# A larger head layout for transposes, a quotient of routing weights, and re-ordered first rounds and layer steps, in a kernel of attention followed by eight experts

## The chip, the cores and the metric

The kernel runs on one core of a Trainium2 chip. The metric is device microseconds (us) of one launch. A core has TensorE (PE in the profile: products, with weight loads on a row of their own, PEld), VectorE (DVE), ScalarE (ACT), GpSimd (POOL, which here mostly issues DMAs) and SyncE (SP, DMAs only). The engines run side by side, each through its own queue in order, and wait for each other by semaphores.

## The reference

Attention over 4 batches, 8 heads, 768 positions of width 64; heads 0, 2 and 6 see all earlier positions, the others only the first 4 and the last 64. The result, as 3,072 tokens of width 512, goes through a dense mixture of 8 experts (hidden width 1,024), weighted by a routing matrix P that is normalized by rows and columns eight times. Condensed:

```python
scores = scale * np.matmul(q, k.transpose(0, 1, 3, 2))
mask = np.where(retr[0, :, 0, 0, None, None], full_mask, stream_mask)
a = np.exp(np.where(mask, scores, -1e9) - max); a = a / a.sum(-1)
x = np.matmul(a, v).transpose(0, 2, 1, 3).reshape(B * S, H * D)
...
P = np.exp(x @ w_gate - max)
for _ in range(8):
    P /= P.sum(1, keepdims=True) + 1e-09
    P /= P.sum(0, keepdims=True) + 1e-09
    P *= N / E
for e in range(E):
    out += P[:, e:e + 1] * (np.maximum(x @ w1[e], 0.0) @ w2[e])
```

## The kernel before

Two stages follow each other, the first to about 177 us.

**Attention and expert 0.** A unit is a batch b, a third of its positions g (256 of them) and a half of the heads u (4 heads): 24 units. GpSimd loads k and q of (b, g) with a cast to 16 bits by `load_kq` (L90), as `[p, h, c, d]`: partition p holds positions 2p + c of each head h, so that a partition's run in memory is 2 x 64 numbers of one head. The first third of batch 0 comes by other queues in 32 bits and is rounded by ScalarE in `round_first` (L167). v of batch 0 comes in the same layout and is put in place by products and copies in `place_v` (L117); v of the other batches comes straight (`load_v_heads`, L133). `emit_prep` (L248) transposes k and q of a unit on TensorE: for each of k and q, pair of heads a and parity c, two products of 64 columns each, one for each head, into the two partition halves of a PSUM tile `tr`; VectorE copies that out as `kT`.

The work of a round is two tasks: scores (`emit_scores`, L427), exponent on ScalarE and mask on VectorE (the pair that `soften` runs), and a round later the sums over v (`gen_pv`, L281), normalized by VectorE into `xn`. `turn` (L312) transposes xn into xT with full products. As soon as xT has a third, expert 0's two layers for it are put in a list of fillers, which `fill` deals out among the rounds. Expert 0's output goes to `acc` unweighted, since P isn't known yet. The first six rounds (L527 to L582) are written out by hand, in the order in which PE, ScalarE and VectorE run them; `make_masks` (L231) builds the masks there, two VectorE operations for each pair of heads, and `warm` (L522) puts in products whose result isn't used. GpSimd's queue has its order by hand only at the start (L395 to L419); its later loads are placed by the planner as buffers come free.

Then P is normalized (L605 to L624), while fillers run.

**Experts 1 to 7.** 42 works (e, c), an expert and a chunk c of 512 tokens. The first work is plain (`layer1_plain`); in the other 41 `layer1` and `layer2` form a product of 2 x 2 blocks from seven block products (Strassen's scheme in Winograd's form): VectorE makes the sums of blocks (S1 and T2 of weights, T1 of xT, S2 of hT), TensorE the seven products, ScalarE copies a bank that is needed again to R (`copy`, L725; R1, R2 and R5, one buffer each), and VectorE adds and cuts at zero in `relu_sum`. A step (g, k) is product k for half g of the hidden width; the pairs at L761 set their order, a pair to a slot. In `layer2` the results times P of this expert go onto acc, by VectorE (L800) or by ScalarE and an adding DMA (L797, L805). `body` deals out slots: a pair of layer 1, a product of layer 2, and pieces of the other generators. `weight_first` (L638) is one of them: in expert 1 it multiplies acc by P of expert 0, four ScalarE operations of 128 x 512 for each chunk, before the first addition to that chunk. VectorE's order is by hand there; ScalarE's follows from the order of issue.

Of the kernel before, what the change touches and what calls it, by code (L numbers as in the profile page):

```python
# [10 lines left out]
F32 = mybir.dt.float32  # L11
# [25 lines left out]
def kernel(  # L37
# [49 lines left out]

    kq, vts = {}, {}

    def load_kq(b, g, h0=0, h1=H):  # L90
        if (b, g) not in kq:
            kq[b, g] = tuple(
                ap.tile([128, H, 2, D], F16, tag=n, bufs=3, name=f"{n}_{b}_{g}")
                for n in ("k16", "q16"))
        for src, dst in zip((k, q), kq[b, g]):
            nc.gpsimd.dma_start(
                out=dst[:, h0:h1].rearrange("p h c d -> p h (c d)"),
                in_=src[b, h0:h1, 256 * g:256 * g + 256, :].rearrange("h (p c) d -> p h (c d)", c=2),
            )

    def v_tile(b):
        if b not in vts:
# [14 lines left out]
    def place_v(g):  # L117

        for n in range(2):
            t = psA.tile([128, 512], F32, tag="mo", bufs=3, name=f"vp_{g}_{n}")  # L120
            rows = slice(64 * n, 64 * n + 64)
            for c in range(2):
                nc.tensor.matmul(
                    out=t[64 * c:64 * c + 64, :].rearrange("p (h d) -> p h d", h=H),
                    lhsT=ident16[rows, rows], rhs=vraw[g][rows, :, c, :], start=True, stop=True,
                )
            dst, src = v_tile(0)[:, :, 2 * g + n, 0:D], t.rearrange("p (h d) -> p h d", h=H)
            if g == 2:
                nc.vector.tensor_copy(out=dst, in_=src)
            else:  # L130
                nc.scalar.activation(out=dst, in_=src, func=AF.Copy, bias=0.0, scale=1.0)
# [34 lines left out]

    def round_first(h0):  # L167
        if (0, 0) not in kq:
            kq[0, 0] = tuple(ap.tile([128, H, 2, D], F16, tag=n, bufs=3, name=f"{n}_0_0")
                             for n in ("k16", "q16"))  # L170
        for i in range(2):
            nc.scalar.activation(out=kq[0, 0][i][:, h0:h0 + 4], in_=first32[:, i, h0:h0 + 4],
                                 func=AF.Copy, bias=0.0, scale=1.0)

    ret_u = constp.tile([128, 2 * H], U32, tag="ret_u")
# [55 lines left out]
    def make_masks(js):  # L231
        for h in [2 * j + hh for j in js for hh in range(2)]:
            nc.vector.tensor_scalar(
                out=masks[h // 2][:, h % 2, :], in0=keep, scalar1=over[:, h:h + 1],
                scalar2=None, op0=ALU.is_gt,
            )
# [11 lines left out]
    def emit_prep(b, g, u):  # L248

        tr = psA.tile([128, 512], F32, tag="mo", bufs=3, name=f"tr_{b}_{g}_{u}").bitcast(F16)  # L250
        for i, src in enumerate(kq[b, g]):
            for a in range(2):
                for c in range(2):
                    for hh in range(2):
                        nc.tensor.transpose(  # L255
                            out=tr[64 * hh:64 * hh + 64, ts(4 * i + 2 * a + c, 128)],
                            in_=src[:, 4 * u + 2 * a + hh, c, :], identity=ident16,
                        )
        t = ap.tile([128, 2, 2, 256], F16, tag=f"kT{u}{g}", bufs=1 + (g == 0),
                    name=f"kT_{b}_{g}_{u}")  # L260
        kTs[b, g, u], qTs[b, g, u] = t[:, 0], t[:, 1]
        nc.vector.tensor_copy(
            out=t.rearrange("r i a (n c p) -> r (i a) c n p", c=2, p=64),
            in_=tr.rearrange("r (i c n p) -> r i c n p", i=4, c=2, p=64),
        )
# [224 lines left out]
    def finish_sums(between=None):  # L490

        for i, ((gen, scale), key) in enumerate([(sums_of[key], key) for key in sums_of]):
            if i and between:
                between()
            while run(gen, 1):
                pass
            del sums_of[key]
            scale[0]()
# [15 lines left out]
    def scores(n):  # L514
        return [emit_scores(*t) for t in tasks[2 * n:2 * n + 2]]

    def soften(pairs, which=(0, 1)):
        for pair in pairs:
            for w in which:
                pair[w]()  # L520

    def warm(n):  # L522

        keep_warm(ident16, kTs[units[0]].rearrange("p a s -> p (a s)"), n)
# [3 lines left out]
    with tc.manual_schedule(engines=engines):  # L528
        keep_warm(blank[:, 0:128], blank, 9)
        make_keep()  # L530
        make_far()
        round_first(0)
        make_masks((0,))
        emit_prep(*units[0])
        make_masks((1,))
        round_first(4)
        r0 = scores(0)
        soften(r0, (0,))
        make_masks((2, 3))
        emit_prep(*preps.pop())  # L540
        warm(2)
        place_v(0)
        soften(r0, (1,))
        sum_later(0)
        r1 = scores(1)
        soften(r1, (0,))
        emit_prep(*preps.pop())
        finish_sums()
        r2 = scores(2)
        soften(r1, (1,))  # L550
        soften(r2, (0,))
        warm(2)
        turn()
        sum_later(1)
        r3 = scores(3)
        place_v(1)
        finish_sums(lambda: emit_prep(*preps.pop()))
        soften(r3, (0,))
        emit_vfar(0, 1)
        soften(r2, (1,))  # L560
        sum_later(2)
        turn()
        r4 = scores(4)
        finish_sums()
        soften(r3, (1,))
        soften(r4, (0,))
        fill(1)
        sum_later(3)
        finish_sums()
        soften(r4, (1,))  # L570
        fill(1)
        r5 = scores(5)
        turn()
        emit_prep(*preps.pop())
        soften(r5, (0,))
        spell_far(2, farx[:, :, 1])
        sum_later(4)
        finish_sums()
        fill(1)
        soften(r5, (1,))  # L580
        sum_later(5)
        fill(1)  # L582
# [15 lines left out]
    emit_logits(B - 1)  # L598
    late[0] = True

    rs = xp.tile([128, NB], F32, tag="rs")
    rr = xp.tile([128, NB], F32, tag="rr")
    bs = xp.tile([128, E], F32, tag="bs")
    rcs = xp.tile([128, E], F32, tag="rcs")
    for it in range(8):  # L605
# [12 lines left out]
        if it == 7:  # L618
# [16 lines left out]
    psB = ctx.enter_context(tc.tile_pool(name="psB", bufs=4, space=bass.MemoryType.PSUM,  # L635
                                         reuse_waits="tile"))

    def weight_first(c):  # L638

        for nb in range(4 * c, 4 * c + 4):  # L640
            nc.scalar.activation(out=acc_of(nb), in_=acc_of(nb), func=AF.Copy,  # L641
                                 bias=0.0, scale=Pne[:, nb, 0:1])
            yield

    works = [(e, c) for e in range(1, E) for c in range(NCH)]
    lefts1, rights1, lefts2, rights2, hTs = {}, {}, {}, {}, {}
# [60 lines left out]
    def layer1(e, c):  # L707
# [50 lines left out]
                                     bias=0.0, scale=1.0)  # L758


        for pair in (((0, 1), (0, 2)), ((0, 5), (0, 6)), ((0, 3), (1, 1)), ((0, 7), (1, 2)),  # L761
                     ((1, 5), (1, 6)), ((0, 4), (1, 7)), ((1, 3), (1, 4))):
            for g, k in pair:
                step(g, k)
            yield
# [8 lines left out]
    def layer2(e, c):  # L774
# [15 lines left out]
        def add(bank, i, n, by_dma):  # L790
            if by_dma:
                t = mp.tile([128, 2, 256], F32, tag="add", bufs=3, name="add")
            for q in range(2):
                dst = acc[c][:, i, n, q, :]
                w = Pne[:, 4 * c + 2 * q + i, e:e + 1]
                if by_dma:
                    nc.scalar.activation(out=t[:, q, :], in_=banks[bank][q], func=AF.Copy,  # L797
                                         bias=0.0, scale=w)
                else:
                    nc.vector.scalar_tensor_tensor(  # L800
                        out=dst, in0=banks[bank][q], scalar=w, in1=dst,
                        op0=ALU.mult, op1=ALU.add,
                    )
            if by_dma:
                nc.gpsimd.dma_start(out=acc[c][:, i, n, :, :], in_=t, accum_op=ALU.add)  # L805
# [51 lines left out]
    def body(n):  # L857
        e, c = works[n]
        if c == 0 and e + 1 < E:
            expw[e + 1] = load_expert(e + 1)  # L860
        if c == 2 and e + 1 < E:
            gens["w"] = combine_w(e + 1)
        if e == 1:
            gens["first"] = weight_first(c)
            gens["x"] = combine_x((c + 1) % NCH)
        for slot in range(7):
            go("l1", 2 if n == 0 and slot == 0 else 1)
            if slot in (1, 5):
                go("w")
                go("x", 2)  # L870
            go("l2")
            if slot in (2, 3, 5, 6):
                go("first")
            if slot in (2, 3):
                go("h")
            if n == 0 and slot == 0:
                run(combine_w(1), 9)
        if n + 1 == len(works):
            gens["l2"] = layer2_last(e, c)
            return  # L880
        gens["h"] = combine_h(e, c)
        go("h", 2)
        gens["l2"] = layer2(e, c)
        gens["l1"] = layer1(*works[n + 1])
# [40 lines left out]
```

The softmax here doesn't subtract the row's maximum and nothing guards it: scores larger than these inputs give would overflow.

## Time and profile before

| | us |
|---|---|
| median of 8 runs | 701.1 |
| lowest, highest | 700.51, 702.83 |
| the profiled execution, whole time | 700.68 |
| its span | 699.0 |

| group in the profile | what it is |
|---|---|
| L255 tr<-ident,k and tr<-ident,q | transposes of keys and queries, 192 products each, median 219 ns |
| L641 acc<-acc,Pne | acc times P of expert 0, ScalarE, 24 of them |
| L727 R<-l1y, R<-l1w | ScalarE's copies of a bank to R, about 600 ns |
| L718, L783 | products of layer 1 and layer 2 of experts 1 to 7 |
| L733 | VectorE's sum and cut at zero, about 685 ns |

Durations of products overlap, as they are pipelined; what a product takes of TensorE's time is read from one start to the next. The profile's clock row shows TensorE's full clock granted all through.

### The profile page before, as it was taken

The page shows a single profiled execution, that of the slowest core. Times are in us where ns is not written, and L with a number is a line of the kernel's source. Part 1 is how long each engine was busy: PE and PEld are TensorE (multiplying, and loading weights), DVE is VectorE, ACT ScalarE, POOL GpSimd, SP SyncE. Part 2 cuts the span into 40 slices and gives each one's busy share as a digit, 9 for nine tenths or more (in the row PEclk, how much of TensorE's full clock was granted, in tenths as well). Part 3 has the DMA queues.
Part 4 walks back from the last instruction along what each step waited for, and adds up shares of the span by engine and source line. Part 5 has one row for each costly group of instructions (what it writes and reads, how often), then busy time and mean ns, then how long its engine had stood idle before and what let it go on. Part 6 is the DMA issues. An engine that isn't in the chain of part 4 may idle for free.

```text
span 699.0 us, 17004 instructions
## 1 busy us (share of the span) xinstructions
PE 684.3 (98%) x6913; PEld 568.6 (81%) x6913; DVE 570.1 (82%) x1149; ACT 419.9 (60%) x775; POOL 151.2 (22%) x183
## 2 busy tenths in 40 slices
PE   7999999999999999999999999999999999999997
PEld 3666666666588888888888888888888888888885
DVE  7785665757889988888888878988898788888785
ACT  6777677774896555655555565555556555555651
POOL 7432220000012131212212121122212212121210
PEclk9999999999999999999999999999999999999999
DMA  9999691000734287346924594349433964245785
GB/s 179 183 192 130 50 76 14 3 1 2 120 61 76 48 129 128 63 76 111 147 47 76 93 151 77 61 68 163 88 62 61 144 114 77 46 76 108 144 163 148
DMA packets 84256, 65.62 MB, mean 94 GB/s; under 512 B 48336, under 2 KB 64720, under 8 KB 84176
## 3 DMA queue, kind: packets, MB, share of 16 engines
q0 software_dynamic: 74976, 57.17, 58.7%
q1 hardware_dynamic: 7552, 6.30, 3.7%
q10 hardware_dynamic: 1648, 1.05, 0.6%
q8 instruction: 54, 0.88, 0.5%
q14 instruction: 26, 0.21, 0.1%
HBM read 52.45 MB, written 6.29 MB: 84 GB/s over the span
## 4 chain that ended last, share of the span: by engine, by line
PE 92%; ACT 4%; DVE 2%; issue 1%; DMA 1%; ACTq 0%
PE l1y L718 20%; PE l2y L783 20%; PE l1w L718 10%; PE l2w L783 10%; PE l L375 6%; PE l1z L718 5%; PE l2z L783 5%; PE l L361 5%; PE sc L454 3%; PE pv L291 3%; ACT PT L463 2%; PE tr L255 2%; PE last L835 1%; PE l1b L698 1%; PE xt L320 1%; ACT acc L641 1%
## 5 line engine op out<-in xcount | busy, mean ns | idle before, releaser
L805 POOL DMA_DIRECT2D acc<-add x120 | 101.4, 845 | 381.0 <-DVE hT L733 182.8
L718 PEld LDWEIGHTS <-S 128*128 128x128 f16 x1312 | 128.3, 98 | 17.2 <-issue 2.1
L783 PEld LDWEIGHTS <-S 128*128 128x128 f16 x1312 | 128.3, 98 | 14.9
L727 ACT ACTIVATE R<-l1y 128x512 f32<-128x512 f32 x164 | 98.5, 601 | 40.5 <-PE l1y L718 40.5
L800 DVE SCALAR_TENSOR_TENSOR acc<-l2y,Pne,acc 128x256 f32<-128x256 f32 x248 | 108.1, 477 | 18.0 <-PE l2y L783 17.9
L718 PEld LDWEIGHTS <-w 128*128 128x128 f16 x984 | 96.3, 98 | 11.4
L783 PEld LDWEIGHTS <-hT 128*128 128x128 f16 x984 | 96.3, 98 | 11.1
L718 PE MATMUL l1y<-T,S 128*128 128x256 f16 x656 | 98.4, 273 | 0.5 <-ACT R L727 0.5
L463 ACT ACTIVATE PT<-sc 128x1024 f16<-128x1024 f32 (+1 forms) x96 | 82.9, 922 | 12.9 <-PE sc L454 12.3
L783 PE MATMUL l2y<-T,S 128*128 128x256 f16 x656 | 85.0, 273 | 0.0
L797 ACT ACTIVATE add<-l2z,Pne 128x256 f32<-128x256 f32 x80 | 33.6, 472 | 77.2 <-PE l2z L783 77.2
L727 ACT ACTIVATE R<-l1w 128x512 f32<-128x512 f32 x82 | 49.2, 599 | 37.6 <-PE l1w L718 37.6
L655 DVE TENSOR_TENSOR S<-hT 128x1024 f16<-128x1024 f16 x82 | 56.2, 686 | 16.4 <-ACT hT L757 14.0
L733 DVE CUSTOM_DVE_ANT_0 hT<-l1w,R 128x512 f16<-128x512 f32 x82 | 56.1, 684 | 7.8 <-PE l1w L718 7.8
L733 DVE CUSTOM_DVE_ANT_0 hT<-l1z,R 128x512 f16<-128x512 f32 x82 | 56.1, 685 | 7.5 <-ACT R L727 7.4
L733 DVE CUSTOM_DVE_ANT_0 hT<-l1y,R 128x512 f16<-128x512 f32 x82 | 56.3, 687 | 4.3 <-PE l1y L718 0.8
L757 ACT ACTIVATE hT<-l1y 128x512 f16<-128x512 f32 x82 | 49.1, 599 | 17.2 <-PE l1y L718 16.0
L797 ACT ACTIVATE add<-l2w,Pne 128x256 f32<-128x256 f32 x80 | 33.6, 472 | 28.1 <-PE l2w L783 27.2
L718 PE MATMUL l1w<-xT,S 128*128 128x256 f16 x328 | 49.2, 273 | 1.1 <-ACT R L727 1.1
L718 PE MATMUL l1y<-xT,w 128*128 128x256 f16 x328 | 49.2, 273 | 0.0
L718 PE MATMUL l1z<-xT,w 128*128 128x256 f16 x328 | 49.2, 273 | 0.0
L718 PE MATMUL l1w<-T,S 128*128 128x256 f16 x328 | 49.2, 273 | 0.0
(106 smaller groups left out, 1043.7 us busy)
## 6 DMA issues: line engine op xcount, KB each, us to landing
acc<-add POOLq DMA_DIRECT2D x120, 256.0 KB, 3.4
w<-in_moe_w_dram POOLq DMA_DIRECT2D x16, 1024.0 KB, 10.4
out_dram<-acc SPq DMA_DIRECT2D x43, 128.0 KB, 2.8
k<-in_k_dram POOLq DMA_DIRECT2D x11, 256.0 KB, 10.7
q<-in_q_dram POOLq DMA_DIRECT2D x11, 256.0 KB, 11.5
v<-in_v_dram POOLq DMA_DIRECT2D x12, 192.0 KB, 11.5
acc<-in_v_dram POOLq DMA_DIRECT2D x3, 256.0 KB, 7.6
acc<-in_q_dram ACTq DMA_DIRECT2D x2, 256.0 KB, 5.4
```

What stands on the lines that cost most here:

```text
L361: nc.tensor.matmul(out=l1[:, ts(fb % 2, 256)], lhsT=w1[:, dc, ts(fb, 128)], rhs=xT[dc // 2][:, dc % 2, c0:c0 + 256], start=(dc == 0), stop ...
L375: nc.tensor.matmul(out=l2, lhsT=hT[fc // 2][:, o:o + 128], rhs=w2[:, fc, :], start=(fc == 0), stop=(fc == 7),)
L463: nc.scalar.activation(out=PT[:, :, c0:c0 + width], in_=sc[:, :, 0:width], func=AF.Exp, bias=0.0, scale=SCALE,)
L655: nc.vector.tensor_tensor(out=out_, in0=a_, in1=b_, op=op)
L718: nc.tensor.matmul(out=banks[g, bank][:, f, :], lhsT=lefts1[e][k - 1][:, dc, ts(2 * g + f, 128)], rhs=rights1[c][k - 1][:, dc, :], start=( ...
L727: nc.scalar.activation(out=R[name], in_=banks[g, bank], func=AF.Copy, bias=0.0, scale=1.0)
L733: nc.vector._custom_dve(TENSOR_ADD_SAT, out=block(g, i, n), in0=banks[g, bank], in1=R[name], s0=65504.0, s1=0.0)
L757: nc.scalar.activation(out=block(g, 1, 0), in_=banks[g, "y"], func=AF.Relu, bias=0.0, scale=1.0)
L783: nc.tensor.matmul(out=banks[bank][q], lhsT=lefts2[e, c][k - 1][:, q, f, :], rhs=rights2[e][k - 1][:, f, :], start=(first and q == 0 and f ...
L797: nc.scalar.activation(out=t[:, q, :], in_=banks[bank][q], func=AF.Copy, bias=0.0, scale=w)
L800: nc.vector.scalar_tensor_tensor(out=dst, in0=banks[bank][q], scalar=w, in1=dst, op0=ALU.mult, op1=ALU.add,)
L805: nc.gpsimd.dma_start(out=acc[c][:, i, n, :, :], in_=t, accum_op=ALU.add)
```

## The change

There are four parts.

1. k and q of all thirds but the second and third of batch 0 are laid out as `[p, c, h, d]`, two heads side by side for each parity. `emit_prep` then transposes two heads by one product of 128 columns. A partition's run in memory becomes 64 numbers. The two thirds left out (`long_runs`) keep layout and products.
2. The first rounds by hand are re-ordered: masks of the last pair later, `place_v(0)` after the scores of round 1, `place_v(1)` before `turn`, the exponents of round 1 apart, one `warm` product in place of four. Of `place_v`'s copies the second (n = 1) goes to VectorE for all thirds.
3. With expert 1, acc isn't multiplied by P of expert 0. Instead expert 1's results are weighted with P1/P0 (`over0`), and acc is multiplied by P0 when expert 2 comes to the chunk. VectorE copies the weights for that to a small tile `wt`, and ScalarE's four operations stand in slots 1 and 2 of expert 2's chunks, one and three.
4. In `layer1` the third and fourth pairs of steps are (1,1), (1,2) and (0,7), (0,3) in place of (0,3), (1,1) and (0,7), (1,2).

```diff
+    def long_runs(b, g):
+        return b == 0 and g in (1, 2)
+
+    def kq_tiles(b, g):
+        shape = [128, H, 2, D] if long_runs(b, g) else [128, 2, H, D]
...
+            if long_runs(b, g):
+                nc.gpsimd.dma_start(out=dst.rearrange("p h c d -> p h (c d)"),
+                                    in_=s.rearrange("h (p c) d -> p h (c d)", c=2))
+            else:
+                nc.gpsimd.dma_start(out=dst, in_=s.rearrange("h (p c) d -> p c h d", c=2))
...
-            if g == 2:
+            if g == 2 or n:
                 nc.vector.tensor_copy(out=dst, in_=src)
...
+                    h, n = 4 * u + 2 * a, 4 * i + 2 * a + c
+                    if not long_runs(b, g):
+                        nc.tensor.transpose(
+                            out=tr[:, ts(n, 128)], identity=ident16,
+                            in_=src[:, c, h:h + 2, :].rearrange("p h d -> p (h d)"),
+                        )
+                        continue
...
         round_first(4)
         r0 = scores(0)
         soften(r0, (0,))
-        make_masks((2, 3))
+        make_masks((2,))
         emit_prep(*preps.pop())
-        warm(2)
+        warm(1)
+        soften(r0, (1,))
+        r1 = scores(1)
+        r1[0][0]()
         place_v(0)
-        soften(r0, (1,))
+        r1[1][0]()
         sum_later(0)
-        r1 = scores(1)
-        soften(r1, (0,))
         emit_prep(*preps.pop())
         finish_sums()
+        make_masks((3,))
         r2 = scores(2)
         soften(r1, (1,))
         soften(r2, (0,))
-        warm(2)
+        place_v(1)
         turn()
         sum_later(1)
         r3 = scores(3)
-        place_v(1)
         finish_sums(lambda: emit_prep(*preps.pop()))
...
+    def weigh_over():
+        nc.vector.reciprocal(out=over0[:, :, 0], in_=Pne[:, :, 0])
+        nc.vector.tensor_tensor(
+            out=over0[:, :, 1:], in0=Pne[:, :, 1:LATE],
+            in1=over0[:, :, 0:1].broadcast_to([128, NB, LATE - 1]), op=ALU.mult)
+
+    def weight_of(e, nb):
+        return (over0 if e < LATE else Pne)[:, nb, e:e + 1]
...
-        for nb in range(4 * c, 4 * c + 4):
-            nc.scalar.activation(out=acc_of(nb), in_=acc_of(nb), func=AF.Copy,
-                                 bias=0.0, scale=Pne[:, nb, 0:1])
-            yield
+        wt = mp.tile([128, 4], F32, tag="wt", name=f"wt_{c}")
+
+        def hold(i0, i1):
+            nc.vector.tensor_copy(out=wt[:, i0:i1], in_=Pne[:, 4 * c + i0:4 * c + i1, 0])
+
+        def weigh(i0, i1):
+            for i in range(i0, i1):
+                x = acc_of(4 * c + i)
+                nc.scalar.activation(out=x, in_=x, func=AF.Copy, bias=0.0, scale=wt[:, i:i + 1])
+
+        hold(0, 1)
+        yield
+        weigh(0, 1)
+        yield
+        hold(1, 4)
+        yield
+        weigh(1, 4)
+        yield
...
-        for pair in (((0, 1), (0, 2)), ((0, 5), (0, 6)), ((0, 3), (1, 1)), ((0, 7), (1, 2)),
+        for pair in (((0, 1), (0, 2)), ((0, 5), (0, 6)), ((1, 1), (1, 2)), ((0, 7), (0, 3)),
...
-                w = Pne[:, 4 * c + 2 * q + i, e:e + 1]
+                w = weight_of(e, 4 * c + 2 * q + i)
...
+        if e == LATE:
+            gens["first"] = weight_first(c)
         if e == 1:
-            gens["first"] = weight_first(c)
             gens["x"] = combine_x((c + 1) % NCH)
         for slot in range(7):
+            if slot in (1, 2):
+                go("first")
             go("l1", 2 if n == 0 and slot == 0 else 1)
+            if slot in (1, 2):
+                go("first")
...
-            if slot in (2, 3, 5, 6):
-                go("first")
...
             if n == 0 and slot == 0:
                 run(combine_w(1), 9)
+                weigh_over()
```

More of the change, by code (lines that the diff above doesn't have):

```diff
@@ L88, with load_kq @@
     kq, vts = {}, {}
[L90 to L94, printed above, removed]
-        for src, dst in zip((k, q), kq[b, g]):
[L96 to L99, printed above, removed]
+    def long_runs(b, g):
+        return b == 0 and g in (1, 2)
+    def kq_tiles(b, g):
+        shape = [128, H, 2, D] if long_runs(b, g) else [128, 2, H, D]
+        kq[b, g] = tuple(ap.tile(shape, F16, tag=n, bufs=3, name=f"{n}_{b}_{g}")
+                         for n in ("k16", "q16"))
+    def load_kq(b, g):
+        kq_tiles(b, g)
+        for src, dst in zip((k, q), kq[b, g]):
+            s = src[b, :, 256 * g:256 * g + 256, :]
+            if long_runs(b, g):
[3 more added lines that the diff above has]
+                nc.gpsimd.dma_start(out=dst, in_=s.rearrange("h (p c) d -> p c h d", c=2))
     def v_tile(b):
@@ L168, in round_first @@
         if (0, 0) not in kq:
-            kq[0, 0] = tuple(ap.tile([128, H, 2, D], F16, tag=n, bufs=3, name=f"{n}_0_0")
-                             for n in ("k16", "q16"))
+            kq_tiles(0, 0)
         for i in range(2):
-            nc.scalar.activation(out=kq[0, 0][i][:, h0:h0 + 4], in_=first32[:, i, h0:h0 + 4],
+            nc.scalar.activation(out=kq[0, 0][i][:, :, h0:h0 + 4].rearrange("p c h d -> p h c d"),
+                                 in_=first32[:, i, h0:h0 + 4],
                                  func=AF.Copy, bias=0.0, scale=1.0)
@@ L253, in emit_prep @@
                 for c in range(2):
+                    h, n = 4 * u + 2 * a, 4 * i + 2 * a + c
[5 more added lines that the diff above has]
+                        continue
                     for hh in range(2):
                         nc.tensor.transpose(
-                            out=tr[64 * hh:64 * hh + 64, ts(4 * i + 2 * a + c, 128)],
-                            in_=src[:, 4 * u + 2 * a + hh, c, :], identity=ident16,
+                            out=tr[64 * hh:64 * hh + 64, ts(n, 128)],
+                            in_=src[:, h + hh, c, :], identity=ident16,
                         )
@@ L599 @@
     late[0] = True
+    LATE = 2
+    over0 = xp.tile([128, NB, LATE], F32, tag="over0")
     rs = xp.tile([128, NB], F32, tag="rs")
```

## The prediction

> **What bounds the kernel now.** I read the page first, then a table by stage, then the chain of waits and the timelines where a stage leaves TensorE idle.
>
> The page (busy time by engine, the slices, the chain that ended last):
> ```profile
> PE 684.3 (98%) x6913; PEld 568.6 (81%) x6913; DVE 570.1 (82%) x1149; ACT 419.9 (60%) x775; POOL 151.2 (22%) x183
> ...
> PE   7999999999999999999999999999999999999997
> ...
> DMA  9999691000734287346924594349433964245785
> ...
> PE 92%; ACT 4%; DVE 2%; issue 1%; DMA 1%; ACTq 0%
> ```
> TensorE is the bound: 684.3 of 699.0 us. There are two ways to gain: fewer or shorter products, or some of the 14.7 us in which it idles. The DMA row is full only for the first 70 us or so.
>
> The table of stages (columns: stretch, length, busy time and instructions of PE, PE's weight loads, VectorE, ScalarE, GpSimd; clock; DMA share; GB/s):
> ```profile
> 0.00:30.00 30.00, 24.13 (x300) 14.52 (x301) 23.31 (x64) 20.02 (x29) 17.26 (x27) 1.00 1.34 183
> 30.00:60.00 30.00, 29.13 (x456) 19.77 (x455) 22.74 (x58) 23.36 (x33) 11.61 (x13) 1.00 1.94 179
> 60.00:90.00 30.00, 29.31 (x429) 20.09 (x426) 19.26 (x48) 21.10 (x31) 9.07 (x10) 1.00 1.17 76
> 90.00:150.00 60.00, 59.43 (x843) 40.15 (x844) 38.55 (x97) 44.94 (x62) 1.77 (x3) 1.00 0.24 22
> ...
> 189.00:201.00 12.00, 11.50 (x105) 10.02 (x104) 9.83 (x20) 12.00 (x25) 2.60 (x3) 1.00 0.26 45
> 201.00:213.00 12.00, 11.76 (x108) 10.31 (x106) 11.82 (x25) 9.77 (x19) 2.42 (x4) 1.00 0.35 62
> 213.00:225.00 12.00, 12.00 (x112) 10.77 (x110) 11.81 (x25) 6.97 (x14) 2.30 (x4) 1.00 0.37 63
> ...
> 300.00:690.00 390.00, 390.00 (x3565) 348.55 (x3564) 334.61 (x614) 215.48 (x440) 85.34 (x101) 1.00 0.57 98
> ```
> Idle time lies in the first 30 us (5.87) and round the start of expert 1. There ScalarE has not a moment free (12.00 of 12), while from 201 VectorE is at 98%. From 300 on PE has no gap at all.
>
> The chain of waits from 186 to 196 (start, us, what):
> ```profile
> 186.35 1.61 ACT acc L641 x3
> ...
> 189.15 1.22 ACT acc L641 x2
> ...
> 190.86 2.06 ACT acc L641 x4
> ```
> and PE's timeline at the stalls there, and at the largest one that the change touches in the start:
> ```profile
> 188.72 0.60 PE L718 MATMUL l1w<-xT,S 128*128 128x256 f16 x4 [0.84 <-ACT R L727]
> 195.05 0.60 PE L718 MATMUL l1y<-T,S 128*128 128x256 f16 x4 [0.50 <-ACT R L727]
> 202.12 0.60 PE L718 MATMUL l1w<-xT,S 128*128 128x256 f16 x4 [0.24 <-ACT R L727]
> ...
> 20.09 0.28 PE L320 MATMUL xt<-ident,xn 128*128 128x128 f16 x2 [0.75 <-DVE xn L305]
> ```
> In all three stalls a product waits for ScalarE to copy a bank (R), and ahead of that copy stand the scalings of acc at L641.
>
> The key and query transposes and, for the full size, those of xn (x8 and x4 are products in the line):
> ```profile
> 130.15 0.41 PE L255 MATMUL tr<-ident,k 128*64 128x128 f16 x8
> 130.39 0.39 PE L255 MATMUL tr<-ident,q 128*64 128x128 f16 x8
> 130.72 0.30 PE L291 MATMUL pv<-vf,PT 128*128 128x65 f16 x4
> ...
> 133.48 0.40 PE L320 MATMUL xt<-ident,xn 128*128 128x128 f16 x4
> 133.72 0.28 PE L291 MATMUL pv<-vf,PT 128*128 128x65 f16 x4
> ```
> From start to start, 16 half-size ones take 130.72 - 130.15 = 0.57 us (36 ns each), 4 full-size ones 0.24 us (60 ns each).
>
> **What the Trainium skill says.** "TensorE: Matmul & The Clock Gate", Part 3: Packing small matmuls, lets small products in different parts of the array run side by side. The trace agrees: a 128-column product of half width advances by 36 ns, a full one by 60. So the 16 halves are not worth 16 full ones, and halving the count doesn't halve the time. The same page, Part 1: The HAM clock gate, has the clock at half until a window of some 3.4 us was busy; here the first transposes last 316 ns and later ones 219. "DMA: Bandwidth & Descriptors", Specifications, asks for at least 512 B per transfer for line rate. The trace agrees in direction: a 256 B packet of k takes 41 ns, a 128 B packet of v 32, so bytes cost more in small packets. "Perfetto Trace Analysis", DVE / Act Engine Instruction, shows a wait queue ahead of the execution FIFO, so a waiting instruction holds what follows; the copies of R behind L641 are that case.
>
> **The change part by part.**
>
> *Full-size transposes.* 20 of 24 units lose 16 half products for 8 full ones: 160 products fewer. 8 x 60 ns = 0.48 against 0.57 us: 0.09 us a unit. Two units lie in the start, which other waits set; 18 follow where PE is 97 to 99% busy, so 18 x 0.09 = 1.6 us. Unknown: xn's products may not have k's pace. Bounds 0.04 and 0.12 a unit (0.7 to 2.2 us); it is nothing if a full one costs what a pair costs, 71 ns. VectorE's copy of tr is unchanged.
>
> Price: each changed k or q DMA goes from 1,024 packets of 256 B to 2,048 of 128 B. v's 1,536 such packets land about 1.55 us apart when the engines are full, k's 1,024 about 1.43; so 2,048 take about 2.07, +0.65 us a DMA. On POOL's queue the order is the old one but for v's second load of batch 1, now behind k and q of the next third, and w2 of expert 1, behind the k and q after that (5 us of transfer out of their way). Landing and first use before: first k, q of batch 1 at 30.5 and 31.9 against 36.1; v by 40.8 against VectorE's 45.4; the third k, q 51.7 and 53.2 against 56.0; everything later over 10 us early. With +0.65 each the tightest land near 33.2, 43.4 and 52.0: cost 0. Issuing one takes GpSimd 0.88 us (k) or 0.96 (v); by that slope 2,048 take some 1.05, with GpSimd 22% busy. If a DMA takes over 0.9 more, the third pair is late, by up to 1 us.
>
> *First rounds.* The last mask pair goes 0.7 us of VectorE later, behind two copies of keys; two v copies move from ScalarE (0.59) to VectorE (0.69); three warm products go; place_v(0) goes behind the scores of round 1, place_v(1) ahead of turn. The wait at 20.09 is set by VectorE's queue (keys' copy, masks, v copy, reciprocal, xn). Into it come one 0.69 copy and out of it go two masks; ScalarE is relieved of 0.6 in front of the exponents. I take 0.1 us gained, bounds -0.4 (gain 0.4) and +1.5: with the warm products gone, a gap of some 0.3 us near 11.5 can make the clock rise one window later. w2 of expert 0, which lands at 28.7 and is used at 29.5, caps a gain at 0.8.
>
> *Expert 1 over expert 0's weight.* 24 scalings at L641 of 0.7 to 0.8 us leave the six chunks of expert 1 for those of expert 2; 12 short VectorE copies (two per chunk) and two operations for the quotient are added. Start to start the three stalls are: 188.72, where the eight products begun at 186.84 end their pace (0.87) at 187.71, so 1.0; 195.05 against 193.95 + 0.44, 0.66; 202.12 against 200.85 + 0.87, 0.40. Sum 2.1. With two or three scalings of 0.6 (start to start) out from ahead of each R copy, these are covered. What is late next is VectorE, which has gaps of 2.0 at 183.9 and of 0.8, 0.8, 0.4 at 195 to 200 to catch up in. I take 2.0 gained, bounds 0.5 and 2.1. In expert 2 ScalarE has a gap of 2.02 us per chunk (at 301.7) and needs 3 x 0.6 there: nothing. The fourth, in front of R1 of the second half, puts that some 0.4 us back, and what waits is a VectorE sum with slack.
>
> *Order of layer 1's steps, 41 chunks.* Product 3 of the first half moves 2.2 us later. Its sum must read R2 before ScalarE writes R2 again, now one slot on: by the steady chunk it ends near 304.6 and the copy starts at 304.91, slack 0.28; in the full chunks of expert 1 it is 0.03. PE has no idle time there to win: gain 0, cost 0 while VectorE stays in time; I put 0.1 in for expert 1.
>
> Sum on the profiled execution's 700.68 us (699.0 span, 1.7 round it): -1.6 - 0.1 - 2.0 + 0.1 = -3.6, so 697.1. That execution lies 0.4 under the median of 701.1, so for the median 697.5.
>
> **Rivals.** 0.2% (1.4 us) is about what a measurement can tell from no change.
> - A. Full-size transposes cost what pairs do, because the strip of two heads is read at a longer stride or its weight load (106 ns on its own engine) shows. For: 60 ns is four products' pace only. Against: weight loads have room there (40.15 of 60). 701.1 - 2.0 = 699.1.
> - B. VectorE takes over between 185 and 250: it is at 11.8 of 12 from 201, so PE catches up into it and gives back 1.9 of the 2.0. Against: its own gaps before 201. 701.1 - 1.7 = 699.4.
> - C (slower). The single R2 buffer: VectorE's sum of product 3 is later than ScalarE's copy wants, and R2's copy, its bank and the next product wait. It repeats in all 41 chunks, where PE has no slack: 0.15 us each is 6.2, so 701.1 - 3.6 + 6.2 = 703.7. It decides from 0.12 us a chunk. For: the slack is 0.28 and VectorE 86% busy there. Against: VectorE waits for PE 0.2 to 0.4 us several times a chunk, so it recovers.
> - D. The start loses: half clock one window longer, or packets dearer than 0.9 us a DMA. 1.5 to 3.5 lost of the 3.6: 699 to 701.
> That the change does not do what it says I rule out by the instructions: the 160 transposes are gone and the scalings stand in expert 2.
>
> **How the numbers follow.** The likeliest case (gains of 2.5 to 4.6, 696.5 to 698.6) 0.58, A 0.10, B 0.11, C 0.11, D 0.10. Range 696.0 to 700.4: down to all gains at their upper bound, up through A, B and half of D; C and the rest stay out. Faster by over 0.2% (under 699.7): 0.58 + 0.08 + 0.07 + 0.05 = 0.78. Within: 0.02 + 0.04 + 0.05 + 0.01 = 0.12. Slower: C, 0.10.
>
> **What would show it.** Transposes: eight products from the first of tr to the next pv in about 0.48 us; in 60 to 150 us the same work ends some 1.5 us sooner. Expert 1: no idle of PE over 0.3 us from 188 to 203, and ScalarE under 11 of 12 there. Layer 1: PE still without a gap from 300 on, a chunk still every 12.2 us; a wait of an R2 copy or of l1w there would be C. Start: xn's second half at or before 20.1. Wrong would be: a transposing product above 70 ns, an engine other than PE at 100% from 189 to 225, or a wait of PE for k, q or kT between 30 and 60.

## The result, and the profile after

The changed kernel takes 696.73 us (median of 10 runs, 696.53 at the lowest) against 701.12 before (28 runs): a ratio of 0.9938, 95% interval 0.9929 to 0.9946, so 4.3 us faster (3.8 to 5.0). Two later sets of five runs gave 697.88 and 697.08. The forecast was 697.5. One of the ten, the one that was profiled, took 1,005 us with TensorE's clock at 0.658 of full speed, so the lines below are from a later execution of the same kernel (697.0 us, span 695.1).

The page of the changed kernel:

```profile
PE 681.2 (98%) x6750; PEld 568.5 (82%) x6750; DVE 575.8 (83%) x1165; ACT 421.4 (61%) x773; POOL 157.9 (23%) x183
...
PE   6999999999999999999999999999999999999997
...
PEclk7999999999999999999999999999999999999999
DMA  9999791000633396437834593349433954245685
...
PE 93%; ACT 3%; DVE 2%; DMA 1%; issue 1%; SPq 0%; DVEq 0%; ACTq 0%
```

163 products are gone, and TensorE is still the bound. Its first slice went from 7 to 6, and its clock row now opens with a 7: in this execution the clock stood at half until 18.0 us. The table of stages of the changed kernel, with columns as before:

```profile
0.00:30.00 30.00, 23.55 (x279) 14.73 (x280) 23.77 (x66) 18.96 (x27) 18.08 (x26) 0.83 1.39 181
30.00:60.00 30.00, 29.10 (x420) 19.99 (x419) 23.11 (x60) 23.96 (x34) 14.50 (x14) 1.00 2.31 170
...
90.00:150.00 60.00, 59.30 (x792) 40.42 (x792) 39.48 (x98) 46.48 (x63) 2.50 (x2) 1.00 0.30 21
...
189.00:201.00 12.00, 12.00 (x112) 10.75 (x111) 11.33 (x23) 6.96 (x14) 2.61 (x3) 1.00 0.37 67
201.00:213.00 12.00, 12.00 (x112) 10.75 (x111) 11.73 (x25) 6.97 (x14) 2.51 (x3) 1.00 0.37 67
213.00:225.00 12.00, 12.00 (x111) 10.65 (x110) 11.71 (x25) 7.08 (x14) 2.53 (x3) 1.00 0.36 66
...
300.00:690.00 390.00, 390.00 (x3551) 347.22 (x3550) 335.98 (x611) 217.28 (x442) 85.35 (x101) 1.00 0.57 100
```

Round the start of expert 1 ScalarE fell from 12.00 to 6.96 of 12 us, and the table shows no idle time of TensorE from 189 on. (Busy times of pipelined products overlap, so pauses of about 0.1 us don't show in it; they are read below from one start to the next.) VectorE went up there from 9.83 to 11.33 and still keeps pace.

To see where the time went, the same events are compared in the traces (us against the kernel before; minus is earlier). Each column is one execution. The 3rd to the 6th copy of kT belong to the two thirds that keep the old layout; l2z is a bank of layer 2's products, so its 17th product lies in expert 1 and its 65th in expert 2:

| event | time before | layout alone | rounds alone | weights alone | step order alone | changed, 1st | changed, 2nd |
|---|---|---|---|---|---|---|---|
| 3rd copy of kT | 14.26 | -0.52 | -0.70 | +0.08 | +0.46 | -0.37 | +0.34 |
| 7th copy of kT | 36.87 | -0.52 | -0.09 | +0.08 | +0.46 | -0.49 | +0.31 |
| start of expert 1 (first hT<-l1b) | 178.40 | -2.78 | -0.08 | +0.10 | +0.46 | -2.74 | -1.93 |
| 17th product of l2z | 217.04 | -2.77 | -0.08 | -2.18 | +0.57 | -5.02 | -4.22 |
| 65th product of l2z | 290.40 | -2.77 | +0.01 | -2.09 | +0.88 | -4.60 | -3.81 |
| first product of the last layer | 687.78 | -2.76 | +0.02 | -2.08 | +0.89 | -4.59 | -3.80 |
| end of the span | 698.97 | -2.77 | -0.10 | -2.08 | +0.87 | -3.01 | -3.89 |

From row to row the changed kernel wins 2.25 and 2.24 us between the start and expert 1, 2.28 and 2.29 in expert 1, and loses 0.42 and 0.41 up to 290. What is left differs between its executions: 0.8 us in the first 15 us, and in the first column 1.6 us behind the last layer, where the last stores (64 KB) landed in 3.9 to 4.0 us instead of 2.3 to 2.5, though the kernel is the same one. Differences of this kind may be why a set of five runs of it spreads over 2 us.

### The profile page after: what moved, and what is told of

The parts are those of the page before. It is cut to its first block, busy times and chain, and to the rows that moved or that the text cites. A ratio compares the mean times of both kernels' runs of the same rounds, so it can differ in the third digit from the quotient of the medians.

```text
span 1001.6 us, 16653 instructions
## 1 busy us (share of the span) xinstructions
PE 991.5 (99%) x6750; PEld 693.7 (69%) x6750; DVE 587.0 (59%) x1165; ACT 430.3 (43%) x773; POOL 157.8 (16%) x183
## 3 DMA queue, kind: packets, MB, share of 16 engines
q10 hardware_dynamic: 1648, 1.05, 0.4%
## 4 chain that ended last, share of the span: by engine, by line
PE 98%; DVE 1%; DMA 0%; ACT 0%; issue 0%
PE l2y L828 21%; PE l1y L763 21%; PE l2w L828 11%; PE l1w L763 11%; PE l L391 6%; PE l L377 6%; PE l1z L763 5%; PE l2z L828 5%; PE sc L470 3%; PE pv L307 3%; PE tr L265 1%; PE last L880 1%; PE l1b L743 1%; PE xt L336 1%; DMA ret_u<-in_is_retrieval_dram 0%; DVE kT L278 0%
## 5 line engine op out<-in xcount | busy, mean ns | idle before, releaser
L763 PEld LDWEIGHTS <-S 128*128 128x128 f16 x1312 | 157.2, 120 | 57.1
L828 PEld LDWEIGHTS <-S 128*128 128x128 f16 x1312 | 157.3, 120 | 56.7
L763 PEld LDWEIGHTS <-w 128*128 128x128 f16 x984 | 118.0, 120 | 43.1 <-issue 0.5
L828 PEld LDWEIGHTS <-hT 128*128 128x128 f16 x984 | 117.9, 120 | 42.5
L763 PE MATMUL l1y<-T,S 128*128 128x256 f16 x656 | 137.4, 348 | 0.0
L828 PE MATMUL l2y<-T,S 128*128 128x256 f16 x656 | 122.3, 348 | 0.0
L763 PE MATMUL l1z<-xT,w 128*128 128x256 f16 x328 | 68.7, 348 | 0.0
L763 PE MATMUL l1y<-T,w 128*128 128x256 f16 x328 | 68.7, 348 | 0.0
L763 PE MATMUL l1w<-T,S 128*128 128x256 f16 x328 | 68.7, 348 | 0.0
L763 PE MATMUL l1y<-xT,w 128*128 128x256 f16 x328 | 68.7, 348 | 0.0
L763 PE MATMUL l1w<-xT,S 128*128 128x256 f16 x328 | 68.7, 348 | 0.0
```

The costliest lines, as they stand in the source:

```text
L763: nc.tensor.matmul(out=banks[g, bank][:, f, :], lhsT=lefts1[e][k - 1][:, dc, ts(2 * g + f, 128)], rhs=rights1[c][k - 1][:, dc, :], start=( ...
L828: nc.tensor.matmul(out=banks[bank][q], lhsT=lefts2[e, c][k - 1][:, q, f, :], rhs=rights2[e][k - 1][:, f, :], start=(first and q == 0 and f ...
```

## The experiments

**The changed kernel once more.**

> The changed kernel once more, for a profile at full clock. My theory: about 697 us, of a gain of 3.6 to 4.4 us some 2.0 round expert 1 (PE idle under 0.3 us from 188 to 203), 1.6 in the transposes (0.09 a unit, stretched over 30 to 150 us), 0.1 in the start. Rival B: PE gains at 188 to 203 but shows waits on VectorE between 203 and 250. Rival A: eight full-size transposes take 0.57 us from start to start.

Measured: 697.88 (696.40 to 698.59), ratio to before 0.9952 (0.9939 to 0.9964). TensorE's waits on ScalarE at 188 to 203 are gone, and after 203 only four pauses of 0.11 us came, treated below. No wait on VectorE came between 203 and 250, so rival B is wrong.

**The layout with full-size transposes alone.** To the kernel before only `long_runs`, `kq_tiles`, the new `load_kq`, `round_first` and `emit_prep` are added:

```diff
+                    if not long_runs(b, g):
+                        nc.tensor.transpose(
+                            out=tr[:, ts(n, 128)], identity=ident16,
+                            in_=src[:, c, h:h + 2, :].rearrange("p h d -> p (h d)"),
+                        )
+                        continue
```

> The layout with full-size transposes alone. My theory: 1.6 us faster (0.7 to 2.2), the first 30 us unchanged. Rival A (a full product costs what a pair does): 0, within 0.3. Denser DMA packets as a cost: slower, with PE waiting for k, q or kT between 30 and 60 us.

Measured: 698.01 us (697.86 to 698.82), ratio 0.9961 (0.9948 to 0.9973): 2.8 us faster, more than my upper bound of 2.2. TensorE's timeline in this kernel:

```profile
127.62 0.40 PE L263 MATMUL tr<-ident,k 128*128 128x128 f16 x4
127.85 0.39 PE L263 MATMUL tr<-ident,q 128*128 128x128 f16 x4
128.07 0.29 PE L305 MATMUL pv<-vf,PT 128*128 128x65 f16 x4
```

Eight full-size transposes take 128.07 - 127.62 = 0.45 us, not 0.48, and not the 0.57 of rival A. By the nanosecond it is 0.457 in nearly every unit, 57 ns each, against 0.570 before: a gain of 0.113 us a unit, 2.03 us for 18 units. From the third copy of kT to expert 1 this execution gains 2.26; where the other 0.2 comes from isn't shown. The other 0.5 us of the difference lies in the first 15 us; at half clock every product dropped may count more, but the start also moves by as much from one execution to the next. TensorE waits nowhere for k, q or kT after 30 us.

**The first rounds alone**, in the old layout: the order of the diff and `if g == 2 or n`.

> The re-ordered first rounds alone (with the second v copies on VectorE), old layout. My theory: 0.1 us faster, between 0.4 faster and 1.5 slower. If the start hid more than I saw, up to 0.8 faster, capped by the landing of w2 at 28.7 us.

Measured: 700.90 us (13 runs), ratio 1.0001 (0.9993 to 1.001): nothing. The trace shows where this execution, the fastest of the 13, lost its lead. After 19 us this execution was 0.8 us ahead (second copy of xT at 19.69 instead of 20.50); at 25 us 0.1. The table of this kernel by microseconds, clock in the third column from the right:

```profile
19.00:20.00 1.00, 0.73 (x8) 0.43 (x10) 1.00 (x4) 0.37 (x2) 0.36 (x1) 0.65 1.82 181
20.00:21.00 1.00, 1.00 (x17) 0.70 (x14) 0.49 (x2) 1.00 (x2) 0.82 (x2) 0.50 1.82 180
21.00:22.00 1.00, 1.00 (x12) 0.80 (x10) 0.53 (x3) 0.96 (x2) 0.73 (x1) 0.50 1.78 191
22.00:23.00 1.00, 1.00 (x12) 0.76 (x10) 0.74 (x3) 0.00 (x0) 0.48 (x1) 0.64 1.36 199
23.00:24.00 1.00, 1.00 (x21) 0.93 (x18) 0.95 (x3) 0.00 (x0) 0.40 (x1) 1.00 1.26 210
```

TensorE's clock went back to half for about 3.4 us: a mean of 0.65 from 19 to 20 is half from 19.3 on, one of 0.64 from 22 to 23 is half until 22.7. That is the length of the window in the Trainium skill, "TensorE: Matmul & The Clock Gate", Part 1: The HAM clock gate. In this execution what was won by waiting less was lost by running slow. Whether the other 12 runs lost it in the same way isn't known.

**Expert 1 over expert 0's weight alone.** `over0`, `weight_of` and the new `weight_first`, called in expert 2.

> Expert 1 over expert 0's weight alone. My theory: 2.0 us faster (0.5 to 2.1), with PE's three stalls at 188 to 203 gone and expert 2 without a gap. Rival B (VectorE becomes the bound): 0.2 to 0.5 faster, with waits on VectorE after 203. If the old step order doesn't bear the new weighting, PE waits appear in expert 2.

Measured: 698.77 us (7 runs), ratio 0.9970 (0.9959 to 0.9981): 2.1 us faster. The stage of the three stalls, with columns as before:

```profile
189.00:201.00 12.00, 12.00 (x112) 10.76 (x110) 11.33 (x24) 6.73 (x14) 2.61 (x3) 1.00 0.37 67
```

ScalarE is busy for 6.73 of 12 us instead of 12.00. Between the start of expert 1 and the 17th product of l2z this kernel wins 2.28 us, as the changed one does. The three stalls are gone, and with them two short pauses, before 200.41 (0.13 us) and 207.88 (0.09 us). The old step order bears the new weighting: expert 2 shows one pause of 0.1 us.

**The changed kernel with the old step order.**

```diff
-        for pair in (((0, 1), (0, 2)), ((0, 5), (0, 6)), ((1, 1), (1, 2)), ((0, 7), (0, 3)),
+        for pair in (((0, 1), (0, 2)), ((0, 5), (0, 6)), ((0, 3), (1, 1)), ((0, 7), (1, 2)),
```

> The changed kernel with the old order of layer 1's steps. In the profile of the changed kernel three chunks round expert 1 and 2 lost 0.11 us each, where product 7 of the second half waited for the copy to R2. My theory (the new order's single R2 and R5 buffers cost that): 0.2 to 0.4 us faster than the changed kernel, no such pauses at 215, 227 and 240. Rival (the new order covers ScalarE's three weightings in expert 2): 0.5 us slower or more, with waits of PE on ScalarE between 225 and 300.

Measured: 696.25 us (696.12 to 697.35), ratio 0.9936 (0.9922 to 0.9950). Between the 17th and the 65th product of l2z it loses 0.00, where the changed kernel loses 0.42; the pauses are gone, and no wait on ScalarE came in expert 2. Later, near 404 us, this execution lost 0.36 once, behind ScalarE waiting for an adding DMA.

**The step order alone**, on the kernel before.

> The new order of layer 1's steps alone, on the kernel before. My theory: within 0.4 us of before; a loss of up to 0.4 where VectorE is full (189 to 250), nothing from 300 on, where a chunk takes 12.22 us as before. Rival C: 0.15 us in each of 41 chunks, 6 us slower.

Measured: 701.68 us (21 runs), ratio 1.0009 (1.0003 to 1.0016): 0.7 us slower. 0.46 of it stood in this execution before anything had changed (the start); 0.42 was lost in expert 1 and 2. TensorE's timeline of this kernel:

```profile
195.51 0.60 PE L718 MATMUL l1y<-T,S 128*128 128x256 f16 x4 [1.16 <-ACT R L727]
208.45 0.60 PE L718 MATMUL l1y<-T,S 128*128 128x256 f16 x4 [0.42 <-ACT R L727]
```

The stall at 188.7 has shrunk to two pauses of 0.17 us each. Those at product 7 of the second half have grown from 0.50 to 1.16 and from next to nothing to 0.42, and three pauses of 0.11 us follow there, at 220.8, 233.1 and 245.4: that product waits for the copy to R2. From 300 on nothing is lost. Rival C is right about the place and wrong about the number of chunks.

**Full-size transposes everywhere**: `long_runs` returns `False`.

> The changed kernel with the new layout and full-size transposes for the two thirds left out too. If a unit gains 0.12 us and DMA has room: 4 x 0.12 = 0.5 us faster than the changed kernel. If the denser packets are dear in the first 30 us: slower, with PE or VectorE waiting for k, q, v or the weights of expert 0 between 13 and 35 us, by 0.5 us or more.

Measured: 700.68 us (21 runs), ratio 0.9996 (0.9989 to 1.0003), so about 4 us slower than the changed kernel. Not for the reason that I named: no data came late. VectorE and GpSimd in this kernel (start, us):

```profile
4.44 1.32 POOL L108 DMA_DIRECT2D k<-in_k_dram  x1
...
5.58 1.44 POOL L108 DMA_DIRECT2D q<-in_q_dram  x1
...
5.87 1.16 DVE L229 CAST farf<-retf 128x8 f16<-128x8 f32 x2
...
8.33 1.59 POOL L108 DMA_DIRECT2D k<-in_k_dram  x1
...
8.70 2.90 DVE L242 TENSOR_SCALAR mask<-keep,over 128x640 f16<-128x640 f16 x1
9.47 1.71 POOL L108 DMA_DIRECT2D q<-in_q_dram  x1
...
12.39 0.67 DVE L278 COPY kT<-tr 128x1024 f16<-128x1024 f16 x1
```

and in the kernel of the next experiment, whose first loads are in long runs as in the changed kernel:

```profile
5.48 0.24 DVE L229 CAST farf<-retf 128x8 f16<-128x8 f32 x2
...
7.18 0.85 DVE L242 TENSOR_SCALAR mask<-keep,over 128x640 f16<-128x640 f16 x2
7.86 0.90 POOL L105 DMA_DIRECT2D k<-in_k_dram  x1
...
8.67 0.69 DVE L278 COPY kT<-tr 128x1024 f16<-128x1024 f16 x1 [0.65 <-PE tr L265]
8.73 0.90 POOL L105 DMA_DIRECT2D q<-in_q_dram  x1
```

With twice the packets GpSimd issues a load in 1.3 to 1.7 us instead of 0.9, and some of VectorE's operations beside it stretch: two casts of 8 elements from 0.24 to 1.16 us, one mask to 2.90 where two took 0.85. From 4.7 to 12.4 us VectorE has hardly a gap; its casts and masks stand ahead of the first copy of kT, which comes at 12.39 us instead of 8.67, 3.7 us late, and stays late.

Not every operation stretches. In the changed kernel (697.0 us) a copy of kT ran beside an issue of 2,048 packets and kept its length:

```profile
14.59 1.23 POOL L108 DMA_DIRECT2D q<-in_q_dram  x1 [0.24 <-PE tr L271]
14.61 0.69 DVE L278 COPY kT<-tr 128x1024 f16<-128x1024 f16 x1 [0.27 <-PE tr L271]
```

So did the products of PT with a mask (0.55 us beside such an issue and away from one). The Trainium skill, "GPSIMD Engine Reference", Specifications, says that GpSimd's SBUF interfaces are shared with VectorE, with contention for VectorE's two-port modes or two SBUF inputs. The casts and masks would fit that if they ran in a two-port mode, which no line shows; the products of PT with a mask read two SBUF inputs and did not stretch. So why just the casts and masks were hit stays open.

**The removed products put back**: `warm(2)` for `warm(1)`, and `warm(2)` ahead of `place_v(1)`.

> The changed kernel with the three removed products whose result isn't used put back in the first rounds. The re-ordered rounds alone stood 0.8 us ahead at 19.3 us and lost 0.7 of it while the granted clock was 0.5 from 19.3 to 22.7. Theory (the clock fell because of the products taken out): full clock from 13 us on and 0.3 to 0.7 us faster than the changed kernel. Rival (the clock's window falls by chance): within 0.3 of it or up to 0.4 slower, the price of the products.

Measured: 696.78 us (696.49 to 697.16), ratio 0.9941 (0.9928 to 0.9953). Half clock lasted to 14.7 us, and no second window of it came. But the changed kernel also had no second window in either of its executions, and its first ended at 15.2 and 18.0. So whether the three products set it isn't settled. Nor is a gain shown: 696.78 us lies within what sets of the changed kernel gave (696.73 to 697.88).

**Four kernels side by side on one chip**, with before at 701.30 (9 runs). First the changed kernel again, as their measure:

> The changed kernel once more, as the measure for the three runs beside it: 696.5 to 698.0 us, with four pauses of PE of about 0.11 us between 210 and 290.

697.08 us (696.82 to 698.73), ratio 0.9945 (0.9933 to 0.9958), with the four pauses. Then two buffers for R2 and R5:

```diff
-            R[name] = mp.tile([128, 2, 256], F32, tag=f"R{name}", bufs=1, name=f"R{name}")
+            R[name] = mp.tile([128, 2, 256], F32, tag=f"R{name}", bufs=1 + (name != "1"), name=f"R{name}")
```

> The changed kernel with two buffers each for R2 and R5. Theory (the pauses come from the copy to R2 waiting for VectorE's sum that still reads R2): no pause where product 7 of the second half starts, 0.3 to 0.45 us faster than the changed kernel. Rival (the copy is late because ScalarE is behind, or the bank is not free): pauses as before, no gain.

Measured: 696.57 us (696.24 to 697.56), ratio 0.9937 (0.9924 to 0.9949). A pause in the changed kernel, from VectorE's, ScalarE's and TensorE's timelines:

```profile
226.88 0.68 DVE L778 CUSTOM_DVE_ANT_0 hT<-l1w,R 128x512 f16<-128x512 f32 x1
...
227.67 0.60 ACT L772 ACTIVATE R<-l1y 128x512 f32<-128x512 f32 x1
...
227.78 0.60 PE L763 MATMUL l1y<-T,w 128*128 128x256 f16 x4
228.32 0.60 PE L763 MATMUL l1y<-T,S 128*128 128x256 f16 x4
```

and the same place with two buffers:

```profile
226.27 0.68 DVE L778 CUSTOM_DVE_ANT_0 hT<-l1w,R 128x512 f16<-128x512 f32 x1
...
226.83 0.61 ACT L772 ACTIVATE R<-l1y 128x512 f32<-128x512 f32 x1
...
227.17 0.60 PE L763 MATMUL l1y<-T,w 128*128 128x256 f16 x4
227.60 0.60 PE L763 MATMUL l1y<-T,S 128*128 128x256 f16 x4
```

In the first, the copy to R2 starts 0.11 us after VectorE's sum from R2 ends (227.56), and the product 0.05 after the copy ends (228.27): 0.54 from product to product. In the second the copy runs beside the sum (226.83, before 226.95), and the products follow at their pace of 0.43. Three of the four pauses are gone; the fourth, at 278, is another wait. So a single buffer is shown to be the cause of those three. R2 is the one that the lines show; R5 got its second buffer in the same run and wasn't tried by itself. The gain shows in the trace (0.33 us up to the 65th product of l2z); in the runs it is not clear, as the two sets overlap.

Then the two parts that gain, and nothing else of the change:

> The layout with full-size transposes and the weighting of expert 1 over expert 0's, and nothing else of the change. If the parts add: 2.8 and 2.1 us, so 4.9 faster than before, 196.1 to 696.5 in the median with before at 701.0 to 701.1; no pauses between 210 and 290. If the re-ordered rounds or the step order are needed to collect these gains: 697 or more.

(In that text 196.1 is a slip for 696.1.) Measured: 695.84 us (695.48 to 696.36), ratio 0.9922 (0.9909 to 0.9936), the fastest of all, 1.2 us under the changed kernel on the same chip, with all five of its runs below all five of that kernel's. The gains of layout and weights add: -2.86 at the start of expert 1, -5.14 from 217 to 300, no pause before 400. This execution then lost 0.7 us once, near 404, as in the fifth experiment:

```profile
402.93 0.84 ACT L837 ACTIVATE add<-l2y,Pne 128x256 f32<-128x256 f32 x2 [1.59 <-DMA acc<-add]
...
404.31 0.60 PE L758 MATMUL l1y<-T,S 128*128 128x256 f16 x4 [0.55 <-ACT R L767]
```

ScalarE waits for an `add` buffer that an adding DMA still reads while the next expert's weights are being loaded (1 MB each), and the copy of R behind it is late. Last, the changed kernel with the old order and the products back:

> The changed kernel with the old step order and the three removed products back in the first rounds. Theory: without the four pauses 0.4 us faster than the changed kernel and nothing from the products, 695.9 to 696.4. Rival (the products hold the clock up and keep the lead of the re-ordered rounds): 695.5 or less.

696.06 us (695.68 to 696.80), ratio 0.9928 (0.9916 to 0.9941), as without the products: the rival of 695.5 is out. This kernel differs from the one with two parts by the first rounds alone, with the products back in them, and the two sets of runs overlap: the new order of the rounds gains nothing here either. Near 404 this execution lost 0.13 us.

## Why the prediction was right, and where not

The time, the sign and the two parts that carry it were right, and so was the mechanism of each. The sum was 3.6; the measured gain is 4.3. That the two lie so near is in part luck: both gains came out larger than forecast (by 0.65 and 0.28 us), and both smaller parts worse (by 0.32 and 0.1), so nearly half of the error cancelled.

- *Full-size transposes*, 1.6 forecast, 2.25 measured: the cost of one was taken from four products' spacing (60 ns), and eight run at 57. That makes 0.113 a unit, near my upper bound of 0.12, and 2.03 for 18 units; 0.2 us is left over.
- *Price of denser packets* on the path of data: 0 forecast, and right. In the changed kernel's first execution the q of a pair lands 1.65 to 2.1 us behind its k (2.07 estimated), k and q of batch 1 at 30.6 and 32.6 us, before they are needed. Issuing took 1.23 to 1.37 us instead of the estimated 1.05. The price that I left out is the one on VectorE's casts and masks. They stand in the first rounds alone, beside the loads of the two thirds left in long runs, so the changed kernel doesn't pay it; with those loads changed it is 3.7 us.
- *First rounds*, 0.1 forecast, nothing measured by themselves. The bounds of -0.4 to +1.5 held. Their reason, a clock that rises later without the products, may hold too, but isn't shown: in the seven executions with the new order in which the record shows the half clock, it first ended at 12.5 to 19.5 us; in the three with the old order, at 12.4, 12.8 and 14.8, and with the products back it was 14.7 in one and nothing was on record in the other. Beside the layout the new order has gained nothing: with it the seventh copy of kT stood between -0.49 and +0.31 us (six executions, the one with full-size transposes everywhere apart), without it at -0.52 and -0.60. Part of that is when the first copy comes; counted from it, the seventh follows after 27.6 to 28.4 us with the new order and 27.8 and 27.9 without.
- *Weights*, 2.0 forecast, 2.28 measured: all of the three stalls, and two short ones. Rival B fell: VectorE, at 94 to 98% from 189 on, had room for the faster pace, as its own gaps before 201 suggested. ScalarE's gap of 2.0 us in expert 2 hid the weightings, as forecast.
- *Step order*, 0.1 loss forecast, 0.42 measured, of which two buffers took back 0.33 in the trace (the pause at 278 stays, and the old order can show one of its kind too, 0.09 at 283.0 with the first rounds alone). The place was named (VectorE's sum from R2 ahead of ScalarE's copy to R2, slack 0.03 us in expert 1), the number of chunks was not: three in a row pay 0.11 each. Rival C's 41 chunks did not come; from 300 on VectorE's slack is enough. No set of runs shows a gain of this part. One thing may speak for it: all three executions with the old order and both gains (the old order put back, the two parts, and the last kernel) waited 1.0 to 1.6 us for the adding DMA near 403 and lost 0.13 to 0.71 of TensorE's time there, while the five with the new order and both gains had such waits of up to 1.8 us, most of them at other places, and lost nothing. Whether it is the order that covers them wasn't tested.

## What to carry to other kernels

Weigh a small product by its spacing in a long run of its kind: taken from a run of four, it came out 5% too dear (60 ns against 57), which is 0.4 us over 18 units. When steps are put in another order, ask for each single buffer how long its last reader ends before its next writer wants to start, where the engines are fullest and not only in the steady part; where that is next to nothing, a second buffer can take the wait away. A change of several parts should be taken apart: here two of four parts are faster than the whole.

## What the runs showed of the hardware

- Some of VectorE's operations can stretch beside a DMA of 2,048 packets that GpSimd issues, though no data is shared: in the first 12 us one mask operation took 2.90 us where two take 0.85, and the issue itself 1.3 to 1.7 us where one of 1,024 packets takes 0.9. Copies of kT (0.69 us) and products with a mask (0.55 us) kept their length beside such issues.
- TensorE's clock can fall back to half for 3.4 us (19.3 to 22.7 us in the first rounds alone). Before it TensorE was busy only 0.28 of the microsecond from 18 to 19, in which ScalarE and VectorE were full. But a stretch as idle wasn't always followed by a fall: in the run with two buffers for R2 and R5 TensorE was busy only 0.14 of the microsecond from 19 to 20, and no second fall came. What set it off isn't shown:

```profile
18.00:19.00 1.00, 0.28 (x2) 0.11 (x2) 0.96 (x4) 1.00 (x2) 0.00 (x0) 1.00 1.79 180
```

- The clock row of the kernel before showed full clock from the beginning, while transposes at 8 us took 316 ns and later ones 219. Where the row shows no change, the durations still have to be looked at.
